# The last batch of a decode kernel passes its second-layer projection and MLP alone, in the form of a turn

## The chip, the cores and the metric

The kernel runs on one core of a Trainium2 chip. The metric is the device time of one execution in microseconds. The core has five engines with queues of their own: PE (matrix multiplication), DVE (vector), ACT (activation functions), POOL (used here for sums over partitions), and SP, which only issues DMA transfers. Inputs lie in HBM and reach the on-chip memory (SBUF) by DMA, over 16 DMA engines; PE writes to PSUM.

## The reference

Two layers are computed one after the other, with the same weights and the same caches in both. A layer is a grouped-query attention block over cached keys and values and a mixer with an MLP, each with a layer norm ahead of it, for 8 batches with one new token each:

```
x = x + A(layernorm(x));  x = x + B(layernorm(x))     # first layer
x = x + A(layernorm(x));  x = x + B(layernorm(x))     # second layer

A: q = x @ wq                       # 448 -> 16 heads x 256
   scores = q . k / 16              # 8 KV heads, two query heads each, 4096 cached tokens
   o = softmax(scores) . v
   return o.reshape(16 * 256) @ wo  # 4096 -> 448
B: ...                              # mixer part: with one token its shifted terms are all zero,
                                    #   so x1 = x
   return x1 + gelu(layernorm(x1) @ w3) @ w4          # 448 -> 1792 -> 448
```

With a sequence of one token each of the mixer's four shifted groups is padded to nothing, so `w1` and `w2` don't touch the output. The batches don't depend on one another. One batch and KV head has 2 MB of keys and 2 MB of values in bfloat16; all of K and V is 256 MB.

## The kernel before

**Slots and loads.** The caches stream through 31 slots of 512 KB (`NSLOT`, 128 partitions of 4 KB). A KV head's keys or values are four chunks of one slot each. `chunks` (L452 to 468) makes the load units: up to `most` neighbouring chunks go in one DMA, so a load has 512 KB, 1 MB or 2 MB, and each partition's part of it is one contiguous row of 4, 8 or 16 KB. All of these loads are issued by SP in one order, `stream`, and each waits until its slots have been read out.

**Pairs of heads.** The work is cut into pairs of KV heads `m` = 0 to 3 of batch `b` in layer 0 or 1. `kpart` computes the scores of a pair: keys are turned either by PE with an eviction by ACT (L856, L916), or by DVE as 32x32 squares (L938); then PE multiplies them with the queries (L926 for the first form, L947 for the second, L975 and L979 for the wide form, which pair 0 of layer 1 has). A softmax over the pair follows (L1004 to L1054), with sums over partitions by POOL. `vpart` passes the values: in the usual form the probabilities are the stationary operand (L1115, with the collecting steps L1126, L1128, L1137, L1141); in the `still` form, used for the last pair of a batch, the values are stationary (L1089, 16 matmuls for each chunk), and the result of each head is normalised by one DVE step (L1096).

**Queries on the diagonal.** For keys turned in squares the queries are needed in a spread form. `diagonal` (L619 to 650) makes it for each pair: a DVE step (`spread`, L633) multiplies eight columns of queries by a mask of quarters, PE sums over partitions with four matmuls of 8 columns each (L640), and another DVE step (`put`, L646) writes the spread queries to one of the two halves of `qe`.

**Turns.** Layer 1 of a batch follows its layer 0 closely: the turned keys of pairs 1 to 3 stay in their slots for it, while pair 0's keys and all values are loaded a second time. Once a batch has all its four pairs of layer 0, `turn(b)` (L652 to 718) takes it to layer 1: output projection (`outproj`, L1155: for each head 16 matmuls of one column, L1163), the residual, the norm (`norm1`, L557), the first MLP layer (`project`, L576: 56 matmuls, L584 and L586), gelu (`gelu`, L590), the second layer (`down`, L602: 56 matmuls, L609), the residual (L678), then the norm and the query projection of layer 1. All of it is for one batch, with one column per operand; scratch lies in `qe` and `small`, and sums in the first columns of the PSUM tile `psT`. Then layer 1 of that batch begins, while the next batch's layer 0 streams.

**The end.** The outputs of layer 1 of all batches gather in `qo`, eight columns (batches) for each head. `outproj8` (L1170) projects a pair for all eight batches at once: 32 matmuls of 8 columns (L1178), called when the last batch's pair has been passed. `end` (L788 to 829) then does the rest for all batches at once: sum of the projections (L797 to 803), `norm8` (L738: L746 to L755), `project` with 8 columns, two roots, `gelu`, `down`, the residual (L814), four transposes back to rows (L821), a copy (L826) and one store of 8 rows (L827). Its scratch is one slot, `U_s1`, handed out after the last load of the stream has its slots.

**Order.** The order on each engine is written by a planner (`Plan.schedule`, L170): every step is an `Op` with an estimated cost, a priority and its dependencies, and the planner lets each engine take the ready step with the lowest priority value. Steps on the same PSUM tile keep the order in which they were added whenever the engine changes. The planner also places the loads: it may split a load of several chunks (`split`, L147) when too few neighbouring slots are free and its estimate of the queue runs low. `end` is added last, with `plan.prio = 1e9`.

For the last batch, `b` = 7, the values go in the order of the pairs 1, 2, 3, 0 (L1267, L1275); pairs 2 and 3 are loaded with up to 2 MB in a DMA, pair 0 with up to 1 MB.

Of the kernel before, what the change touches and what calls it, by code (L numbers as in the profile page):

```python
# [3 lines left out]
P = 128  # L4
B = 8
D = 448
# [354 lines left out]
def bass_interleave_layers__gqa_block_cached__mixer_s_mlp__decode_kernel(  # L361
# [90 lines left out]
    def chunks(cache, b, h, name, skip=(), most=2):  # L452
# [123 lines left out]
    def project(w, wt, half, j0, j1, rhs, out0, nb, units, bufs, name, cost=None):  # L576


        def emit(e):
            last = None  # L580
            for j in range(j0, j1):
                o = psT[:, out0 + j * nb:out0 + (j + 1) * nb]
# [36 lines left out]
    def diagonal(layer, b, m):  # L619
# [11 lines left out]
        def spread(e):  # L631
            src = psT[:, 64 + 8 * m:72 + 8 * m] if layer else qo[:, 8 * m:8 * m + 8, b]
            return e.tensor_tensor(qm.rearrange("p (q x) -> p q x", q=4), src.unsqueeze(1).to_broadcast([P, 4, 8]),  # L633
                                   quarter.unsqueeze(2).to_broadcast([P, 4, 8]), ALU.mult)
        dve(spread, 180, [Bsel] + ([] if layer else [Bq1[b]]), Bqe[k], [bT] if layer else [], name=n + "m")

        def emit(e):
            for c in range(2):
                for h in range(2):
                    last = e.matmul(part.rearrange("p (n c q h) -> p c h q n", c=2, q=4, h=2)[:, c, h],  # L640
                                    same[:, :], qm.rearrange("p (q n h c) -> p c h q n", q=4, h=2, c=2)[:, c, h], start=True, stop=True)
            return last
        add("pe", emit, 140, Bqe[k] + [Bsel], [], [bT], name=n + "s")
# [8 lines left out]
    def turn(b):  # L652

        n = f"turn{b}"
        keep, plan.prio = plan.prio, -1.0
# [3 lines left out]
        last = ahead[[a[0] for a in ahead].index(b)]  # L659
        ahead.remove(last)  # L660
        dve(lambda e: e.tensor_reduce(sjk[:, :], psT[:, 0:24].rearrange("p (s c) -> p c s", c=4), axis=AX.X, op=ALU.add),
            180, [], [Bs["jk"]], [bT], name=n + "ao")
        dve(lambda e: e.tensor_tensor(sjk[:, :], sjk[:, :], x[:, 0:4], ALU.add), 150, [Bs["jk"], Bx[b]], [Bs["jk"]], name=n + "xa")
        outproj(*last, [0])
        dve(lambda e: e.tensor_tensor(sjk[:, :], psT[:, 24:28], sjk[:, :], ALU.add), 150, [Bs["jk"]], [Bs["jk"]], [bT], name=n + "xb")
        plan.turn = True
        outproj(*last, [1])
        dve(lambda e: e.tensor_tensor(sx1[:, 0:4], psT[:, 28:32], sjk[:, :], ALU.add), 150, [Bs["jk"]], [Bs["x1"]], [bT], name=n + "x1")
# [11 lines left out]

        norm1(x, Bx[b], Bx4[b], 41, n + "b")
# [21 lines left out]
        def columns(r):  # L703
            def emit(e):
                for j in range(4):
                    last = e.matmul(psT[:, 64 + 16 * r:80 + 16 * r].rearrange("p (g j) -> p j g", j=4)[:, j],
# [61 lines left out]
    def start():  # L768
# [12 lines left out]
        for i in range(4):  # L781
            project(wq_sb, wqt_sb, 16, 8 * i, 8 * i + 8, rhs, 64, 8, U_wq + wq_rest + [U_s0], [byn], f"sq{i}")
# [5 lines left out]
    def end():  # L788
        w = Wide(U_s1)
# [7 lines left out]
        dve(lambda e: e.tensor_reduce(ao(), psT[:, 0:192].rearrange("p (s c) -> p c s", c=32), axis=AX.X, op=ALU.add),  # L797
            400, [], [bao], [bT], units=u, name="eao")
        dve(lambda e: e.tensor_tensor(ao(), ao(), xT[:, 0:4, :].rearrange("p c b -> p (c b)"), ALU.add), 200, [bao] + Bx, [bao], units=u, name="exa")
# [3 lines left out]
        dve(lambda e: e.tensor_tensor(x1()[:, 0:32], psT[:, 224:256], ao(), ALU.add), 200, [bao, b1], [b1], [bT], units=u, name="ex1")  # L803
# [23 lines left out]
        U_out = plan.load(Unit("out", lambda e, _: e.dma_start(out[:, 0, :], xo()[0:B, :]), 8192, slotted=False),  # L827
# [597 lines left out]
```

## Time and profile before

| | before |
|---|---|
| median of 3 runs | 1095.2 us (1094.35 to 1099.57) |
| the profiled execution | 1096.3 us, its span 1094.5 us |
| PE busy | 764.3 us (70%), 15416 matmuls |
| DVE busy | 830.5 us (76%) |
| ACT, POOL busy | 212.2 us (19%), 72.0 us (7%) |
| moved by DMA | 448.96 MB, mean 410 GB/s |
| mean granted TensorE clock | 0.616 |

The profile is that of one execution. Its span runs from the first to the last recorded instruction, and the execution's own time is 1.8 us longer. "Busy" counts the time in which an engine worked on an instruction; weight loads of PE (PEld) overlap its matmuls. In the timelines the first column is the start in microseconds from the span's start, the second the length; square brackets give the idle time of the engine before it and who ended it. A line number is that of the kernel before.

### The profile page before, as it was taken

The page shows a single profiled execution, that of the slowest core. Times are in us where ns is not written, and L with a number is a line of the kernel's source. Part 1 is how long each engine was busy: PE and PEld are TensorE (multiplying, and loading weights), DVE is VectorE, ACT ScalarE, POOL GpSimd, SP SyncE. Part 2 cuts the span into 40 slices and gives each one's busy share as a digit, 9 for nine tenths or more (in the row PEclk, how much of TensorE's full clock was granted, in tenths as well). Part 3 has the DMA queues.
Part 4 walks back from the last instruction along what each step waited for, and adds up shares of the span by engine and source line. Part 5 has one row for each costly group of instructions (what it writes and reads, how often), then busy time and mean ns, then how long its engine had stood idle before and what let it go on. Part 6 is the DMA issues. An engine that isn't in the chain of part 4 may idle for free.

```text
span 1094.5 us, 33709 instructions
## 1 busy us (share of the span) xinstructions
PE 764.3 (70%) x15416; PEld 525.1 (48%) x15416; DVE 830.5 (76%) x1567; ACT 212.2 (19%) x322; POOL 72.0 (7%) x232
## 2 busy tenths in 40 slices
PE   3467586778677865778667786578766795676865
PEld 3255453465346543565336654365433654346533
DVE  5899549964997499954999569974799839996572
ACT  1023131113011311203202032121221231111310
POOL 0000000000000000000000010000100000000000
PEclk9998566556655665556655566555565666655655
DMA  9999999999999999999999999999999999999994
GB/s 357 405 420 417 411 400 428 422 404 409 428 422 417 411 428 426 422 395 423 426 426 419 399 423 426 426 416 398 427 428 424 400 406 426 426 423 414 416 425 188
DMA packets 54703, 448.96 MB, mean 410 GB/s; under 512 B 5520, under 2 KB 11552, under 8 KB 14112
## 3 DMA queue, kind: packets, MB, share of 16 engines
q1 hardware_dynamic: 54400, 446.42, 98.3%
q8 instruction: 121, 1.98, 0.7%
q10 hardware_dynamic: 160, 0.38, 0.1%
q14 instruction: 22, 0.18, 0.0%
HBM read 446.77 MB, written 0.01 MB: 408 GB/s over the span
## 4 chain that ended last, share of the span: by engine, by line
DVE 39%; DMA 26%; PE 20%; issue 7%; ACT 3%; POOL 1%; SPq 0%; DVEq 0%; POOLq 0%
DVE slots L938 31%; DMA slots<-in_A_k_cache_dram 17%; DMA slots<-in_A_v_cache_dram 9%; PE psV L1115 5%; PE psS L947 4%; DVE pT L1045 2%; PE psS L926 2%; PE psV L1089 2%; PE psT L609 1%; ACT slots L916 1%; DVE slots L1128 1%; PE psT L695 1%; PE psT L1163 1%; PE psK L856 1%; ACT slots L1217 1%
## 5 line engine op out<-in xcount | busy, mean ns | idle before, releaser
L938 DVE STREAM_TRANSPOSE slots<-slots 128x1024 bf16<-128x1024 bf16 x544 | 647.7, 1230 | 38.2 <-DMA slots<-in_A_k_cache_dram 25.1
L947 PE MATMUL psS<-qe,slots 128*128 128x8 bf16 x5760 | 225.4, 174 | 165.2 <-DVE slots L938 107.5
L947 PEld LDWEIGHTS psS<-qe,slots 128*128 128x128 bf16 x5760 | 190.5, 103 | 250.1 <-DVE slots L938 173.0
L1115 PE MATMUL psV<-slots,pT 128*8 128x512 bf16 x1528 | 183.7, 555 | 20.0 <-DMA slots<-in_A_v_cache_dram 15.2
L916 ACT COPY slots<-psK 128x1024 bf16<-128x1024 bf16 x80 | 78.6, 1015 | 165.1 <-PE psK L856 164.6
L856 PE MATMUL psK<-ident,slots 128*128 128x128 bf16 x640 | 75.1, 304 | 3.1 <-DMA slots<-in_A_k_cache_dram 2.9
L1009 POOL PARTITION_ALL_REDUCE small<-small x64 | 23.9, 374 | 720.4 <-DVE small L1007 586.0
L1126 ACT ACTIVATE slots<-psV 128x512 bf16<-128x512 f32 x48 | 28.8, 600 | 201.9 <-PE psV L1115 201.9
L856 PEld LDWEIGHTS psK<-ident,slots 128*128 128x128 bf16 x640 | 62.4, 141 | 5.7 <-DMA slots<-in_A_k_cache_dram 3.5
L975 PE MATMUL psS<-slots,qe 128*8 128x512 bf16 x200 | 55.3, 593 | 6.5 <-DVE slots L938 6.4
L1089 PE MATMUL psV<-pT,slots 128*128 128x2 bf16 x1568 | 50.6, 165 | 9.6 <-DMA slots<-in_A_v_cache_dram 9.0
L1115 PEld LDWEIGHTS psV<-slots,pT 128*8 128x8 bf16 x1528 | 31.5, 90 | 52.6 <-DMA slots<-in_A_v_cache_dram 21.5
L1089 PEld LDWEIGHTS psV<-pT,slots 128*128 128x128 bf16 x1568 | 47.2, 104 | 11.6 <-DMA slots<-in_A_v_cache_dram 9.1
L1128 DVE TENSOR_TENSOR slots<-psV,slots 128x512 bf16<-128x512 f32 x48 | 32.5, 677 | 25.2 <-ACT slots L1126 25.0
L1030 ACT ACTIVATE pT<-psS 128x128 bf16<-128x128 f32 x56 | 15.6, 279 | 173.6 <-DVE psS L1027 173.4
L1045 DVE STREAM_TRANSPOSE pT<-psS 128x128 bf16<-128x128 bf16 x64 | 45.2, 706 | 4.4 <-PE psS L1037 2.2
L1137 PE MATMUL psV<-same,slots 128*128 128x4 bf16 x320 | 14.2, 166 | 41.9 <-DVE slots L1128 36.8
L1163 PE MATMUL psT<-small,wo_sb 128*128 128x1 bf16 x1024 | 35.7, 166 | 7.1 <-DVE small L1096 4.7
L926 PE MATMUL psS<-qo,slots 128*128 128x2 bf16 x768 | 28.0, 167 | 13.4 <-ACT slots L916 10.4
L1163 PEld LDWEIGHTS psT<-small,wo_sb 128*128 128x128 bf16 x1024 | 32.5, 105 | 9.2 <-DVE small L1096 6.0
L1137 PEld LDWEIGHTS psV<-same,slots 128*128 128x128 bf16 x320 | 11.8, 103 | 49.6 <-issue 42.3
L1096 DVE TENSOR_TENSOR small<-psV,small 128x4 bf16<-128x4 f32 x30 | 4.3, 144 | 41.1 <-PE psV L1089 41.1
(178 smaller groups left out, 768.8 us busy)
## 6 DMA issues: line engine op xcount, KB each, us to landing
slots<-in_A_v_cache_dram SPq DMA_DIRECT2D x149, 1024.0 KB, 9.9
slots<-in_A_v_cache_dram SPq DMA_DIRECT2D x50, 2048.0 KB, 21.1
slots<-in_A_k_cache_dram SPq DMA_DIRECT2D x45, 2048.0 KB, 21.1
slots<-in_A_k_cache_dram SPq DMA_DIRECT2D x69, 1024.0 KB, 14.3
slots<-in_A_v_cache_dram SPq DMA_DIRECT2D x14, 512.0 KB, 8.0
wo_sb<-in_A_wo_dram SPq DMA_DIRECT2D x4, 896.0 KB, 19.1
wq_sb<-in_A_wq_dram SPq DMA_DIRECT2D x3, 1024.0 KB, 11.3
w_sb<-in_B_w_dram SPq DMA_DIRECT2D x1, 1568.0 KB, 15.2
```

The costliest lines, as they stand in the source:

```text
L856: last = e.transpose(tile[:, j * P:(j + 1) * P], slots[u.slot][:, o:o + P], ident[:, :])
L916: return e.copy(slots[u.slot][:, 1024 * t:1024 * t + 1024], tile)
L926: last = e.matmul(o, slots[u.slot][:, i:i + P], q, start=(cc == 0), stop=(cc == 1))
L938: return e.transpose(o, i)
L947: last = e.matmul(o, slots[u.slot][:, i:i + P], qe[:, 128 * k + 64 * s + 8 * g:128 * k + 64 * s + 8 * g + 8], start=(g == 0), stop=(g == 7))
L975: last = e.matmul(o, q, K[:, lo:hi + 1:hi - lo, :, g, :], start=(g == 0), stop=(g == 7))
L1045: add("dve", lambda e: e.transpose(pZ[:, :, 0:3:2].rearrange("p n s r -> p n r s"), psS[x][:, 128:192].bitcast(bf).rearrange("p (n r s) -> ...
L1089: last = e.matmul(o, slots[u.slot][:, i:i + P], w, start=(c == 0 and cc == 0 and j == 0), stop=(c == NCH - 1 and cc == 1 and j == 7))
L1115: last = e.matmul(psV[x][32 * i:32 * i + 8, :].rearrange("p (k d) -> p k d", k=2), w, v, start=(s == 0 and c == 0), stop=(s == 1 and c == ...
L1126: add("act", lambda e: e.activation(part(0), psV[x][:, :], ACT.Copy), 590, [], [Bhalf[0]], [bV[x]], [v], prio=at - 1, name=n + "ve0").targ ...
L1128: add("dve", lambda e: e.tensor_tensor(part(1), psV[x][:, :], part(0), ALU.subtract), 590, [Bhalf[0]], [Bhalf[1]], [bV[x]], [v], prio=at - ...
L1163: last = e.matmul(psT[:, 4 * (2 * s + i) + c:4 * (2 * s + i) + c + 1], wo_sb[:, a, d0:d0 + P], o1[b % 2][:, a:a + 1], start=(k == 0), stop ...
```

## The change

The second layer's projection and MLP, so far done in `end` for eight batches at the very end, are cut in two.

- `end` now takes its projection by `outproj8` for all four pairs in one place, and is called before the last batch's pairs 2, 3 and 0 are passed, with priority -0.7 in place of 1e9. It still works on eight columns; the last one holds nothing of use then, and only 7 rows are stored. It hands back its scratch slot.
- The last batch's outputs are projected by `outproj` with one column, read from `qo`, to columns of `psT` from `LAST` = 448 on. The body of `turn` up to the residual becomes the function `block`, with a base column, and the new function `end1` calls it for batch 7, transposes the result back to a row, copies it and stores it. SP waits for both stores.
- In `chunks`, the second head of pair 0 of the last batch is loaded in four DMAs of 512 KB instead of two of 1 MB.
- `diagonal` sums with one matmul of 32 columns instead of four of 8. For that the columns of the queries are kept in another order within each four (`swapped`), and `spread` writes its product in another order. The planner's cost of the step goes from 140 to 60.

```diff
-            if len(group) == most:
+            if len(group) == most and not name.startswith(f"B{B - 1}m0V1"):
                 plan.load(group[0], mates=group[1:])
...
+    def swapped(j):
+        return j // 4 * 4 + j % 2 * 2 + j // 2 % 2
...
-            return e.tensor_tensor(qm.rearrange("p (q x) -> p q x", q=4), src.unsqueeze(1).to_broadcast([P, 4, 8]),
-                                   quarter.unsqueeze(2).to_broadcast([P, 4, 8]), ALU.mult)
+            return e.tensor_tensor(qm.rearrange("p (x q h) -> p x q h", x=4, q=4),
+                                   src.rearrange("p (x h) -> p x h", h=2).unsqueeze(2).to_broadcast([P, 4, 4, 2]),
+                                   quarter.unsqueeze(1).unsqueeze(3).to_broadcast([P, 4, 4, 2]), ALU.mult)
...
-            for c in range(2):
-                for h in range(2):
-                    last = e.matmul(part.rearrange("p (n c q h) -> p c h q n", c=2, q=4, h=2)[:, c, h],
-                                    same[:, :], qm.rearrange("p (q n h c) -> p c h q n", q=4, h=2, c=2)[:, c, h], start=True, stop=True)
-            return last
-        add("pe", emit, 140, Bqe[k] + [Bsel], [], [bT], name=n + "s")
+            return e.matmul(part, same[:, :], qm, start=True, stop=True)
+        add("pe", emit, 60, Bqe[k] + [Bsel], [], [bT], name=n + "s", n=1)
...
-    def turn(b):
+    def block(b, n, last, base):
...
-        outproj(*last, [0])
+        outproj(*last, [0], base)
...
+    def turn(b):
+        n = f"turn{b}"
+        keep, plan.prio = plan.prio, -1.0
+        x = xT[:, :, b]
+        last = ahead[[a[0] for a in ahead].index(b)]
+        ahead.remove(last)
+        block(b, n, last, 0)
...
-        outproj8(*late, [0])
-        dve(lambda e: e.tensor_tensor(ao(), psT[:, 192:224], ao(), ALU.add), 200, [bao], [bao], [bT], units=u, name="exb")
-        outproj8(*late, [1])
+        for m in range(HKV // 2):
+            outproj8(m, m, plan.prio)
...
-        U_out = plan.load(Unit("out", lambda e, _: e.dma_start(out[:, 0, :], xo()[0:B, :]), 8192, slotted=False),
-                          after=bxo.writers)
-        return U_out
+        late.append(plan.load(Unit("out", lambda e, _: e.dma_start(out[0:B - 1, 0, :], xo()[0:B - 1, :]), 7168, slotted=False),
+                              after=bxo.writers))
+        return w
+
+    def end1(w, last):
+        plan.prio = -1.0
+        block(B - 1, "f", last, LAST)
+        xo, bxo = w.tile(bf, D), Buf()
+        def back(e):
+            for cc in (3, 0, 1, 2):
+                d0 = cc * P if cc < 3 else D - P
+                t = e.transpose(psT[0:1, 0:224].bitcast(bf)[:, d0:d0 + P], xT[:, cc, B - 1:B], ident[:, :])
+            return t
+        add("pe", back, 400, [Bx[B - 1], Bc], [], [bT], name="fback", n=4)
+        dve(lambda e: e.tensor_copy(xo()[0:1, :], psT[0:1, 0:224].bitcast(bf)), 450, [], [bxo], [bT], units=[U_s1], name="fxo")
+        late.append(plan.load(Unit("outl", lambda e, _: e.dma_start(out[B - 1:B, 0, :], xo()[0:1, :]), 1024, slotted=False),
+                              after=bxo.writers))
...
-                q = q.rearrange("p (s c) -> p s c", c=2)[:, :, cc]
+                q = q[:, 2 * cc:2 * cc + 2]
...
-                late.extend((m, s, at[0] + 1))
+                late.append((b, m, s, -0.5))
             else:
-                outproj8(m, s, at[0] + 1)
+                outproj(b, m, s, at[0] + 1, (0, 1), LAST)
...
+            keep, plan.prio = plan.prio, -0.7
+            W = end()
+            plan.prio = keep
             for m in (2, 3, 0):
                 weave(V(1, b, m, most=4 if m else 2))
-    plan.prio = 1e9
-    U_out = end()
+    end1(W, next(x for x in late if isinstance(x, tuple)))
```

More of the change, by code (lines that the diff above doesn't have):

```diff
@@ L574, in norm1, with project @@
         root(lambda: sf[:, 2:3], lambda k: sf[:, (1, 1, 3, 4)[k]:(2, 2, 4, 5)[k]], None, [Bs["sq"]], [Bs["f"]], [], name + "n", True)
-    def project(w, wt, half, j0, j1, rhs, out0, nb, units, bufs, name, cost=None):
+    def swapped(j):
+        return j // 4 * 4 + j % 2 * 2 + j // 2 % 2
+    def project(w, wt, half, j0, j1, rhs, out0, nb, units, bufs, name, place=lambda j: j):
         def emit(e):
@@ L581, in emit @@
             for j in range(j0, j1):
-                o = psT[:, out0 + j * nb:out0 + (j + 1) * nb]
+                o = psT[:, out0 + place(j) * nb:out0 + (place(j) + 1) * nb]
                 for k in range(3):
@@ L705, in emit @@
                 for j in range(4):
-                    last = e.matmul(psT[:, 64 + 16 * r:80 + 16 * r].rearrange("p (g j) -> p j g", j=4)[:, j],
+                    last = e.matmul(psT[:, 64 + 16 * r:80 + 16 * r].rearrange("p (g j) -> p j g", j=4)[:, swapped(j)],
                                     slots[v.slot][:, 512 * r + P * j:512 * r + P * j + P],
@@ L1162, in emit @@
                         a = 8 * m + 4 * i + k
-                        last = e.matmul(psT[:, 4 * (2 * s + i) + c:4 * (2 * s + i) + c + 1], wo_sb[:, a, d0:d0 + P],
-                                        o1[b % 2][:, a:a + 1], start=(k == 0), stop=(k == 3))
-                return last
-            add("pe", emit, 430, [Bo1[b % 2][m][i]], [], [bT], U_wo, prio=prio, name=f"W{b}m{m}{i}", n=16)
-    late = []
+                        last = e.matmul(psT[:, base + 4 * (2 * s + i) + c:base + 4 * (2 * s + i) + c + 1], wo_sb[:, a, d0:d0 + P],
+                                        qo[:, a, b:b + 1] if base else o1[b % 2][:, a:a + 1], start=(k == 0), stop=(k == 3))
+                return last
+            add("pe", emit, 430, [Bo2[m][i] if base else Bo1[b % 2][m][i]], [], [bT], U_wo, prio=prio, name=f"{'WX'[base > 0]}{b}m{m}{i}", n=16)
+    late, LAST = [], 448
     def outproj8(m, s, prio, heads=(0, 1)):
@@ L1273, in bass_interleave_layers__gqa_block_cached__mixer_s_mlp__decode_kernel @@
         else:
+            keep, plan.prio = plan.prio, -0.7
+            W = end()
+            plan.prio = keep
             for m in (2, 3, 0):
                 weave(V(1, b, m, most=4 if m else 2))
-    plan.prio = 1e9
-    U_out = end()
+    end1(W, next(x for x in late if isinstance(x, tuple)))
+    U_out = [x for x in late if not isinstance(x, tuple)]
     order = U_side[:1] + U_even[:1] + U_side[1:] + U_even[1:] + [U_s0] + stream[:1] + U_wq + stream[1:10] + U_wo + stream[10:]
     order.append(U_s1)
-    order.append(U_out)
+    order += U_out
     seq = plan.schedule(order, NSLOT)
@@ L1374, in run @@
         if e == "sp":
-            eng.wait_ge(U_out.sem, U_out.val)
+            for u in U_out:
+                eng.wait_ge(u.sem, u.val)
     with nc.Block() as blk:
```

25 lines of the change are left out of this document (10 added, 15 removed).

## The prediction

> **What bounds the kernel now.** I read the page first, then the windows of the last 45 us, then the timeline of the end, and last the timeline of a turn, because the change puts a turn's form at the end.
>
> ```profile
> span 1094.5 us, 33709 instructions
> ...
> PE 764.3 (70%) x15416; PEld 525.1 (48%) x15416; DVE 830.5 (76%) x1567; ACT 212.2 (19%) x322; POOL 72.0 (7%) x232
> ...
> DMA  9999999999999999999999999999999999999994
> ...
> DVE 39%; DMA 26%; PE 20%; issue 7%; ACT 3%; POOL 1%; SPq 0%; DVEq 0%; POOLq 0%
> ```
>
> The 16 DMA engines are busy in tenths of 9 in every slice but the last, while PE is at 70%. So the kernel is one stream of cache loads, and its time is the moment at which the last load lands plus what must still be computed after it. The chain names DVE first, but where the stream is never dry a DVE step only matters if it keeps a load from being issued.
>
> The windows show how the stream ends (columns: window, length, busy us of PE, weight loads, DVE, ACT and POOL with their counts, granted clock, DMA share, GB/s):
>
> ```profile
> core 0: us, PE busy (x) PEld busy (x) DVE busy (x) ACT busy (x) POOL busy (x), PEclk, DMA share, GB/s
> 1050.00:1057.00 7.00, 2.51 (x28) 0.77 (x28) 6.91 (x8) 0.96 (x3) 0.00 (x0) 0.50 1.01 426
> 1057.00:1065.00 8.00, 7.21 (x97) 3.70 (x93) 2.26 (x8) 1.06 (x3) 0.83 (x3) 0.69 1.00 426
> 1065.00:1075.00 10.00, 4.38 (x72) 1.81 (x72) 1.18 (x4) 0.93 (x2) 0.07 (x1) 0.69 1.00 419
> 1075.00:1082.50 7.50, 4.73 (x152) 4.42 (x152) 1.80 (x6) 0.16 (x1) 0.00 (x0) 0.50 0.59 244
> 1082.50:1092.80 10.30, 5.78 (x168) 5.07 (x168) 4.93 (x33) 0.30 (x1) 0.41 (x1) 0.50 0.01 4
> ```
>
> The DMA share is 1.00 until 1075 and 0.59 in the 7.5 us after; in the last 10.3 us the DMA is idle (0.01) and PE, DVE and one ACT step take turns. That last stretch is what the change is about. A share of 0.59 with loads still landing also says that some engines are through before others, so the last landing is that of the slowest. In the timeline of it (start, length, engine, line, operation, count, idle before and releaser):
>
> ```profile
> 1080.05 1.01 PE L1089 MATMUL psV<-pT,slots 128*128 128x2 bf16 x32 [0.56 <-DMA slots<-in_A_v_cache_dram]
> ...
> 1082.51 1.01 PE L1089 MATMUL psV<-pT,slots 128*128 128x2 bf16 x32 [1.44 <-DMA slots<-in_A_v_cache_dram]
> 1083.55 0.18 DVE L1096 TENSOR_TENSOR qo<-psV,small 128x4 bf16<-128x4 f32 x1 [3.77 <-PE psV L1089]
> ...
> 1083.79 0.59 PE L1178 MATMUL psT<-qo,wo_sb 128*128 128x8 bf16 x16 [0.27 <-DVE qo L1096]
> 1084.49 0.19 DVE L803 TENSOR_TENSOR slots<-psT,slots 128x32 bf16<-128x32 f32 x1 [0.75 <-PE psT L1178]
> ...
> 1089.80 1.66 PE L609 MATMUL psT<-slots,w_sb 128*128 128x8 bf16 x56 [2.60 <-DVE slots L599]
> 1091.49 0.19 DVE L814 SCALAR_TENSOR_TENSOR slots<-psT,slots 128x32 bf16<-128x32 f32 x1 [1.75 <-PE psT L609]
> ...
> 1091.74 0.59 PE L821 MATMUL psT<-ident,slots 128*8 128x128 bf16 x4 [0.28 <-DVE slots L814]
> 1092.36 0.38 DVE L826 COPY slots<-psT 8x448 bf16<-8x448 bf16 x1 [0.68 <-PE psT L821]
> 1092.82 0.31 SPq L827 DMA_DIRECT2D out_dram<-slots  x1
> ```
>
> The last two megabytes of V are passed at 1080.05 and 1082.51, each waiting for its DMA; the landings are 2.46 us apart. After the last one everything is a single chain: 32 matmuls of the last pass, the normalisation by the softmax sum (L1096), 16 matmuls of the output projection (L1178), the sum (L803), norm and first MLP layer, the second layer (L609), the residual (L814), four transposes, a copy and the store. From 1082.51 to the end of the span at 1094.5 this tail is 12.0 us, 1.1% of the time. No edit of the tail alone can bring more than that.
>
> **Part 1, the tail in a turn's form.** The kernel already runs this chain for one batch in every turn. Here is the last turn (PE rows of L1163 are the output projection, L609 the second MLP layer, L678 the residual):
>
> ```profile
> 1013.02 0.16 DVE L1096 TENSOR_TENSOR small<-psV,small 128x4 bf16<-128x4 f32 x1 [3.17 <-PE psV L1089]
> ...
> 1013.24 0.58 PE L1163 MATMUL psT<-small,wo_sb 128*128 128x1 bf16 x16 [0.26 <-DVE small L1096]
> ...
> 1013.75 0.60 PE L1115 MATMUL psV<-slots,pT 128*8 128x512 bf16 x4
> ...
> 1014.28 0.27 PE L531 MATMUL psT<-qe,small 128*128 128x1 bf16 x4
> ...
> ```
>
> ```profile
> 1018.18 1.65 PE L609 MATMUL psT<-qe,w_sb 128*128 128x1 bf16 x56 [0.23 <-DVE qe L599]
> ...
> 1019.87 0.18 DVE L678 SCALAR_TENSOR_TENSOR small<-psT,qe 128x4 bf16<-128x4 f32 x1 [1.75 <-PE psT L609]
> ```
>
> From L1096 to the residual the turn takes 1019.87 - 1013.02 = 6.85 us; the eight-batch form takes 1091.49 - 1083.55 = 7.94 us. The difference is 1.09 us. It comes from fewer and shorter DVE steps (128x1 in place of 128x8, a scalar operand in place of a broadcast one); the second layer's 56 matmuls are no shorter (1.65 against 1.66), so PE gives nothing here. In the turn another pass of 4 matmuls (1013.75) lies ahead of L531 and costs at most 0.1 us, which the end doesn't have; I leave it as slack. After the residual the steps stay: four transposes (now one row instead of eight, still 128 columns each), a copy of 448 columns, a store; 1094.5 - 1091.49 = 3.01 us, taken unchanged. Term: **-1.1 us**, between -1.2 (slack gained) and -0.6 (half of it lost to steps placed otherwise).
>
> **Part 2, the last head's V in four loads.** The last load is now half as large, so after the last landing 16 matmuls remain instead of 32. By the row at 1082.51 the 32 take 1.01 us, some 27 ns each beyond the first (0.17 by the median of a single small matmul below), so 16 fewer are **-0.4 us**. Against it stands what smaller packets cost in the stream. Each load is one row per partition, so 2 MB that went as 8 KB packets now go as 4 KB packets (512 of them). One answer per window of 4 us, each with its count under 8 KB: calm (994), the three with many 4 KB packets (1010, 486, 878), and one with none that is slow all the same (866):
>
> ```profile
> DMA packets 231, 1.67 MB, mean 418 GB/s; under 512 B 28, under 2 KB 28, under 8 KB 28
> ```
>
> ```profile
> DMA packets 287, 1.54 MB, mean 384 GB/s; under 512 B 33, under 2 KB 33, under 8 KB 168
> ```
>
> ```profile
> DMA packets 266, 1.41 MB, mean 351 GB/s; under 512 B 35, under 2 KB 35, under 8 KB 156
> ```
>
> ```profile
> DMA packets 357, 1.59 MB, mean 398 GB/s; under 512 B 42, under 2 KB 42, under 8 KB 285
> ```
>
> ```profile
> DMA packets 193, 1.38 MB, mean 344 GB/s; under 512 B 25, under 2 KB 25, under 8 KB 25
> ```
>
> Calm is 418 GB/s. The window at 878 holds 285 - 42 = 243 packets of 4 KB (1.0 MB) and loses 20 of 418, 0.19 us per MB, so 0.4 us for 2.1 MB. The one at 1010, the nearest in time, holds 135 and loses 34 of 418 over 4 us, 0.33 us for 0.55 MB, which would be 1.2 us. The one at 486 holds 121 and would give 2.7 us. But 866 falls to 344 with not one such packet, so part of each dip is the turn's and not the packets'. The lower end is nothing. I take **+0.4 us**, from the window with most such packets, and keep 0 to 1.2 for the range and 2.7 for a rival. The two further issues, the split 2 MB load and the second store lie on SP, which issues nothing between the last load and the store at 1092.82: nothing, and with that cover gone 0.3 us each.
>
> **Part 3, batches 0 to 6 earlier.** What was the tail for eight columns is now run beside the last loads, and the last batch's projections are made anew for one column: 128 more matmuls (four times the 1.0 us of 32 such) and, by the last window, 5.78 - 1.01 - 0.59 = 4.2 us of PE and 4.9 us of DVE that come ahead of the last landing. In the instruction order of the changed kernel 96 of those matmuls stand ahead of the last batch's final transposes' scores, near 1040 to 1045, the rest and the norm from the last batch's wide scores on, after 1057. From 1057 to 1082.5 PE is busy 7.21 + 4.38 + 4.73 of 25.5 us and DVE 5.24 of 25.5: 9.2 us and 20 us are free. What could be late next are the loads: those that wait for a slot behind these steps. The last of them is already in the queue long before:
>
> ```profile
> slots<-in_A_v_cache_dram SPq DMA_DIRECT2D x1, 1024.0 KB, 29.6
> ```
>
> It is issued 29.6 us ahead of its landing, so a release that comes 1 to 3 us later (3 us of PE at 1040, one DVE memset that waits for PE) is swallowed. The other thing behind the moved steps is the last softmax, whose chain shares DVE and PE with them:
>
> ```profile
> 1061.05 0.69 DVE L1004 TENSOR_REDUCE small<-psS 128x1 f32<-128x512 f32 x1 [3.61 <-PE psS L979]
> ...
> 1064.56 0.72 DVE L1045 STREAM_TRANSPOSE pT<-psS 128x128 bf16<-128x128 bf16 x1
> ...
> ```
>
> ```profile
> 1075.21 0.99 PE L1089 MATMUL psV<-pT,slots 128*128 128x2 bf16 x32 [0.70 <-DMA slots<-in_A_v_cache_dram]
> ```
>
> It ends at 1065.3 and is first needed at 1075.21; some ten DVE steps of 0.2 us and 56 matmuls of 1.7 us in its way use 4 of these 10 us. Term: **0**; without that cover it would be up to 4.2 us of PE work.
>
> **Part 4, the diagonal.** One matmul of 32 columns takes the place of four of 8, in 64 places, and the spreading step gets a view of four dimensions:
>
> ```profile
> L640 PE MATMUL psT<-qe,same x256: 169/174/221, 25.2 to 1038.9; 128*128 128x8 bf16 x128
> ```
>
> ```profile
> L633 DVE TENSOR_TENSOR qe<-psT,small x32: 151/192/193, 148.3 to 1038.6; 128x32 bf16<-128x32 f32 x32
> ```
>
> ```profile
> L646 DVE TENSOR_TENSOR qe<-psT,small x64: 250/292/442, 26.2 to 1040.0; 128x128 bf16<-128x128 f32 x64
> ```
>
> On PE that is three of 174 ns fewer, pipelined 0.10 us, 64 times: 6.7 us off an engine with 30% idle. On DVE the step of 0.19 us stays between its present minimum 0.15 and the 0.29 of the wider four-dimensional step. Only in the turns are two such chains in series with the queries, so at most 8 x 2 x 0.1 = 1.6 us, if the stream followed every turn. But its loads are held by passes and score matmuls of many kinds, so I take **0**, with -1.6 and (0.1 us lost on DVE in the same 16 places) +1.6 as ends. The planner also orders some steps otherwise from the first batch on, since it counts this step as shorter; I price that as a rival.
>
> **Sum.** -1.1 - 0.4 + 0.4 + 0 + 0 = -1.1 us. The profiled execution took 1096.3 us (span 1094.5 and 1.8 around it), 1.1 above the median of the three runs, 1095.2. On the profile's own time the sum gives 1095.2, and on the median **1094.1**.
>
> **Rivals.** First, on the other side: the small loads cost more than they save. The place is the last 2 MB, the price 2.7 us by the window at 486, and from 1.5 us on it cancels the whole gain. That ends at 1095.2 - 1.5 + 2.7 = 1096.4, slower than before. Against it: the landings at 1080.05 and 1082.51 are as far apart as 1 MB at 418 to 428 GB/s needs, so a queued load shows no price of its own. The Trainium skill speaks against this edit in "DMA: Bandwidth & Descriptors", section "Measured (HBM→SBUF, 128 partitions, SWDGE, issued from GpSimd)": loads should be batched to 1 MiB or more, and the fit in that page's section "Anatomy of one DMA — SWDGE (gpsimd) path" gives each transfer about 2.0 us beside its bytes. By that fit as an estimate two more loads would be +4 us and the kernel would end at 1097.7. The trace's 2.46 us per queued megabyte doesn't bear the fixed part out.
>
> Second: the new order lets the queue of loads run thinner in the turns. A dip as at 866 costs 4 x (418 - 344) / 418 = 0.7 us; one more in four of eight turns is 2.8 us, 1096.9. For it: these dips exist. Against: nearly all loads keep their sizes and places in SP's order.
>
> Third: the turns follow the shorter diagonal and the new order helps. With the full 1.6 us it is 1092.5.
>
> Fourth: the change doesn't do what it says, because the work for batches 0 to 6 is still in PE's and DVE's queues when the last load lands. Up to 4.2 us come back, 1098.3. Against it are the free 9.2 us of PE, and that after each landing PE needs 1.0 of 2.46 us, so a backlog shrinks.
>
> **How the numbers follow.** Forecast 0.60 (1093.0 to 1095.3, from the ends of parts 1 and 2), small loads 0.12, thinner queue 0.11, quicker turns 0.12, late work 0.05. The likeliest gives 1094.1. The range takes in the first three rivals and leaves out late work and mishaps beyond them: 1091.5 to 1097.3. A change of 0.5%, 5.5 us, is about what a measurement of this kernel can tell from nothing; the gain is a fifth of that. Below 1089.7 only a turn effect three times the bound would lead: 0.03. Above 1100.7 only late work together with thinner queues: 0.04. That leaves 0.93.
>
> **What would show it.** Right: the store is issued 8.6 to 9.2 us after the start of the last pass (now 1092.82 - 1082.51 = 10.31); the last pass has 16 matmuls; from the last normalisation by the softmax sum to the residual it takes 6.7 to 6.9 us; the copy of rows 0 to 6 ends before the last landing; the last landing stays within 1 us of 1082.5. Wrong: the last landing moves by more than 1.5 us either way, a pass starts late with its data landed, or the windows of the turns show other GB/s. Then it is the stream and not the tail that decided.

## The result, and the profile after

| | before | after |
|---|---|---|
| median | 1095.42 us (21 runs, 1094.32 to 1100.16) | 1092.94 us (21 runs, 1092.07 to 1095.14) |
| ratio | | 0.9977, 95% interval 0.9969 to 0.9985 |
| the profiled execution | 1096.3 us, span 1094.5 | 1092.74 us, span 1090.9 |

The change takes 2.5 us off (1.6 to 3.4 by the interval), 0.23%. The forecast was a gain of 1.1 us. The lines of the page, the windows of the end and the timeline of the tail, all of the changed kernel, in the columns told ahead of the prediction's:

```profile
span 1090.9 us, 33799 instructions
...
PE 767.1 (70%) x15448; PEld 523.3 (48%) x15448; DVE 834.3 (76%) x1597; ACT 212.4 (19%) x323; POOL 72.2 (7%) x233
...
DVE 34%; DMA 32%; PE 21%; issue 6%; SPq 4%; ACT 3%; POOL 0%; DVEq 0%; POOLq 0%
```

```profile
1050.00:1057.00 7.00, 2.55 (x55) 1.18 (x48) 6.45 (x10) 0.99 (x3) 0.01 (x1) 0.94 0.99 413
1057.00:1065.00 8.00, 8.00 (x132) 4.79 (x130) 3.06 (x15) 0.95 (x2) 0.58 (x2) 0.50 1.02 433
1065.00:1075.00 10.00, 9.53 (x199) 5.73 (x196) 4.84 (x30) 1.49 (x3) 0.77 (x3) 0.50 0.99 407
1075.00:1082.50 7.50, 5.26 (x179) 5.01 (x178) 1.89 (x8) 0.00 (x0) 0.00 (x0) 0.50 0.36 143
1082.50:1092.80 10.30, 4.16 (x120) 3.62 (x120) 3.48 (x26) 0.21 (x1) 0.40 (x1) 0.50 0.01 2
```

```profile
1066.13 0.74 DVE L1067 STREAM_TRANSPOSE pT<-psS 128x128 bf16<-128x128 bf16 x1
...
1072.46 0.31 SPq L833 DMA_DIRECT2D out_dram<-slots  x1
...
1074.23 0.72 PE L1111 MATMUL psV<-pT,slots 128*128 128x2 bf16 x21
...
1075.52 0.43 PE L1111 MATMUL psV<-pT,slots 128*128 128x2 bf16 x11 [0.57 <-issue]
...
1078.61 0.48 PE L1111 MATMUL psV<-pT,slots 128*128 128x2 bf16 x13
...
1080.34 1.09 PE L1111 MATMUL psV<-pT,slots 128*128 128x2 bf16 x35 [1.24 <-issue]
1081.47 0.18 DVE L1118 TENSOR_TENSOR qo<-psV,small 128x4 bf16<-128x4 f32 x1 [2.45 <-PE psV L1111]
...
1081.70 0.58 PE L1185 MATMUL psT<-qo,wo_sb 128*128 128x1 bf16 x16 [0.27 <-DVE qo L1118]
...
1086.43 1.66 PE L613 MATMUL psT<-qe,w_sb 128*128 128x1 bf16 x56 [1.43 <-DVE qe L603]
1088.12 0.17 DVE L677 SCALAR_TENSOR_TENSOR small<-psT,qe 128x4 bf16<-128x4 f32 x1 [1.75 <-PE psT L613]
...
1088.35 0.59 PE L846 MATMUL psT<-ident,small 128*1 128x128 bf16 x4 [0.27 <-DVE small L677]
1088.98 0.38 DVE L849 COPY slots<-psT 1x448 bf16<-1x448 bf16 x1 [0.68 <-PE psT L846]
1089.38 0.25 SPq L850 DMA_DIRECT2D out_dram<-slots  x1
```

Lines have moved with the edit: L1111 is now the last pass (L1089), L1118 the normalisation by the softmax sum (L1096), L1185 the output projection of one batch, L613 the second MLP layer, L677 the residual, L1067 the last softmax's final step (L1045).

From the normalisation (1081.47) to the residual (1088.12) it takes 6.65 us, where the eight-batch form took 7.94 and the turn 6.85. From the residual to the end of the span it is 2.78 us instead of 3.01. So the chain behind the last pass is 1.52 us shorter. The rows of batches 0 to 6 are stored at 1072.46, well ahead of the last landing. PE's busy time between 1057 and 1075 went from 11.6 to 17.5 us and DVE's from 3.4 to 7.9: that is the moved work. But the span is 3.6 us shorter, so about 2 us lie ahead of the chain. Windows of half a microsecond show when the stream ends, first in the kernel before, then in the changed one (the last column is GB/s):

```profile
1081.50:1082.00 0.50, 0.00 (x0) 0.00 (x0) 0.00 (x0) 0.00 (x0) 0.00 (x0) 0.50 0.04 16
1082.00:1082.50 0.50, 0.00 (x0) 0.00 (x0) 0.00 (x0) 0.00 (x0) 0.00 (x0) 0.50 0.00 0
```

```profile
1079.00:1079.50 0.50, 0.10 (x4) 0.01 (x1) 0.02 (x1) 0.00 (x0) 0.00 (x0) 0.50 0.04 16
1079.50:1080.00 0.50, 0.00 (x0) 0.00 (x0) 0.00 (x0) 0.00 (x0) 0.00 (x0) 0.50 0.00 0
```

In these two executions the stream ended about 2.5 us sooner. With the 1.5 us of the chain that would be 4.0; some 0.4 us of it is missing, and PE stood still for 1.24 us ahead of 1080.34.

### The profile page after: what moved, and what is told of

Its sections match the earlier page's. It is cut to its first block, busy times and chain, and to the rows that moved or that the text cites. A ratio compares the mean times of both kernels' runs of the same rounds, so it can differ in the third digit from the quotient of the medians.

```text
span 1090.9 us, 33799 instructions
## 1 busy us (share of the span) xinstructions
PE 767.1 (70%) x15448; PEld 523.3 (48%) x15448; DVE 834.3 (76%) x1597; ACT 212.4 (19%) x323; POOL 72.2 (7%) x233
## 4 chain that ended last, share of the span: by engine, by line
DVE 34%; DMA 32%; PE 21%; issue 6%; SPq 4%; ACT 3%; POOL 0%; DVEq 0%; POOLq 0%
DVE slots L960 26%; DMA slots<-in_A_k_cache_dram 20%; DMA slots<-in_A_v_cache_dram 13%; PE psV L1137 6%; PE psS L969 4%; SPq L434 3%; DVE pT L1067 2%; PE psS L948 1%; PE psV L1111 1%; ACT slots L938 1%; DVE slots L1150 1%; PE psT L613 1%; PE psT L702 1%; PE psS L997 1%; SPq L459 1%
## 5 line engine op out<-in xcount | busy, mean ns | idle before, releaser
L1111 PE MATMUL psV<-pT,slots 128*128 128x2 bf16 x1568 | 50.8, 165 | 7.3 <-DMA slots<-in_A_v_cache_dram 5.0
L1111 PEld LDWEIGHTS psV<-pT,slots 128*128 128x128 bf16 x1568 | 47.4, 104 | 8.8 <-DMA slots<-in_A_v_cache_dram 5.9
L1067 DVE STREAM_TRANSPOSE pT<-psS 128x128 bf16<-128x128 bf16 x64 | 45.4, 710 | 5.2 <-PE psS L1059 2.8
L1185 PE MATMUL psT<-small,wo_sb 128*128 128x1 bf16 x1024 | 35.1, 166 | 7.1 <-DVE small L1118 5.1
L638 DVE TENSOR_TENSOR qe<-psT,small 128x32 bf16<-128x32 f32 x32 | 5.9, 185 | 41.6 <-PE psS L969 37.0
L1185 PEld LDWEIGHTS psT<-small,wo_sb 128*128 128x128 bf16 x1024 | 32.1, 104 | 9.3 <-DVE small L1118 6.4
```

The costliest lines, as they stand in the source:

```text
L1067: add("dve", lambda e: e.transpose(pZ[:, :, 0:3:2].rearrange("p n s r -> p n r s"), psS[x][:, 128:192].bitcast(bf).rearrange("p (n r s) -> ...
L1111: last = e.matmul(o, slots[u.slot][:, i:i + P], w, start=(c == 0 and cc == 0 and j == 0), stop=(c == NCH - 1 and cc == 1 and j == 7))
L1185: last = e.matmul(psT[:, base + 4 * (2 * s + i) + c:base + 4 * (2 * s + i) + c + 1], wo_sb[:, a, d0:d0 + P], qo[:, a, b:b + 1] if base els ...
```

## The experiments

Times are given against the kernel before, run on the same chip; a ratio of 0.999 is 1.1 us.

### The whole change again, and without the new diagonal

Run e1_after_again is the changed kernel unedited. Run e2_old_diagonal takes the diagonal back and leaves the rest:

```diff
-            return e.matmul(part, same[:, :], qm, start=True, stop=True)
-        add("pe", emit, 60, Bqe[k] + [Bsel], [], [bT], name=n + "s", n=1)
+            for c in range(2):
+                for h in range(2):
+                    last = e.matmul(part.rearrange("p (n c q h) -> p c h q n", c=2, q=4, h=2)[:, c, h],
+                                    same[:, :], qm.rearrange("p (q n h c) -> p c h q n", q=4, h=2, c=2)[:, c, h], start=True, stop=True)
+            return last
+        add("pe", emit, 140, Bqe[k] + [Bsel], [], [bT], name=n + "s")
```

The views of `spread` and of the scores and the order of the columns go back too.

> The changed kernel as it is, beside the others on one chip, as the yardstick. Both theories expect 2.5 us below the kernel before (ratio 0.9977). In its profile: from the last normalisation by the softmax sum to the end of the span 9.4 us where the kernel before has 10.95.

> The changed kernel with the diagonal as before: four matmuls of 8 columns, the old order of columns and the planner's old cost; the new tail and the four small loads stay. Tail theory (the gain is the shorter chain after the last landing, 1.5 us, and the half pass, 0.4 us, the rest is chance): 1.9 to 2.5 us below the kernel before, the same as the yardstick within 0.5 us. Stream theory (the tail gives 1.9 us less a price of the small loads, and the diagonal with the planner's new order brings the stream forward by 1 us or more in the turns): only 0.9 to 1.5 us below the kernel before, 1 us or more above the yardstick.

Measured: e1 0.9973 (0.9963 to 0.9984), median 1092.97; e2 0.9984 (0.9973 to 0.9994), median 1093.92, 1.8 us below the kernel before. Tail and loads carry a good part of the gain, and without the diagonal about 1 us of it is missing. The 1.8 us lie just under what the tail theory expected (1.9 to 2.5), and the distance to e1, 1.2 us by the ratios and 1.0 by the medians, is what the stream theory expected; the two intervals overlap. In e1 it is 9.5 us from the last normalisation (1080.75) to the end of the span, where 9.4 was expected.

### The new diagonal alone, its order and its step apart

Three runs start from the kernel before. e3_diagonal_only has the new diagonal and the planner's new cost; e5_new_diagonal_old_order has the new instructions with the old cost, which gives the old order on every engine; e6_planner_cost_only has the old instructions with the new cost, which gives the order of e3:

```diff
 e3: new views, one matmul
-        add("pe", emit, 140, Bqe[k] + [Bsel], [], [bT], name=n + "s")
+        add("pe", emit, 60, Bqe[k] + [Bsel], [], [bT], name=n + "s", n=1)
 e5: new views, one matmul; the line of add as before
 e6: old views, four matmuls; the line of add as in e3
```

> The kernel before with the new diagonal alone (one matmul of 32 columns, the new order of columns, the planner's new cost); tail and loads as before. Tail theory: no change, within 0.4 us of the kernel before. Stream theory: 0.8 to 1.6 us below it, and in its profile the norms of the turns come 1.5 to 3 us sooner, as in the changed kernel.

> The kernel before with the new diagonal's instructions, but the planner keeps its old cost, so every engine's order is the old one. The new diagonal with the planner's new cost alone gained about 2 us. If that gain is the shorter step itself (three small matmuls fewer in the turns, at most 1.6 us), this run has it too: 1.0 to 2.0 us below the kernel before. If it is the order, this run is within 0.5 us of the kernel before.

> The kernel before with its old diagonal of four matmuls, but the planner counts it as 60 and one matmul, so the order on every engine is that of the run with the new diagonal alone. If the order is what gained there: 1.0 to 2.0 us below the kernel before. If the shorter step: within 0.5 us of the kernel before, or above it by the 0.1 us of each step that the planner now doesn't count.

Measured: e3 0.9982 (0.9973 to 0.9990), 2.0 us below; e5 0.9983 (0.9973 to 0.9992), 1.9 us below; e6 1.0023 (1.0010 to 1.0036), 2.5 us above. In the traces DVE, ACT and POOL run through the same sequence of steps in e6 as in e3, and in e5 as in the kernel before, so the orders are those that the text says. The new instructions gain by themselves, in either order. The order gains nothing: with the old instructions behind it, it loses.

Where the stream gained can be read from a fixed point near its end, the sum over partitions of the last turn's second norm. It is the same POOL step in the kernel before, e5, e2 and the changed kernel, one row each:

```profile
1021.34 0.40 POOL L572 PARTITION_ALL_REDUCE small<-small  x1 [5.61 <-DVE small L568]
```

```profile
1019.66 0.40 POOL L572 PARTITION_ALL_REDUCE small<-small  x1 [5.64 <-DVE small L568]
```

```profile
1021.65 0.40 POOL L572 PARTITION_ALL_REDUCE small<-small  x1 [5.60 <-DVE small L568]
```

```profile
1018.45 0.40 POOL L572 PARTITION_ALL_REDUCE small<-small  x1 [5.86 <-DVE small L568]
```

With the new diagonal it comes 1.7 us (e5) and 2.9 us (changed) sooner, with the old diagonal in the changed kernel no sooner (e2, 0.3 later). In e3 it comes at 1019.41, 1.9 us sooner, as the stream theory expected. Over all executions, the four kernels with the old diagonal have this step at 1021.17 or later, and six of the seven whose diagonals all have one matmul have it between 1018.45 and 1019.66; the seventh is e12, the run with many small loads below, with 1021.08. Each is a single execution, so one row proves nothing alone.

The view of SP's own waits shows where the diagonal can hold up a load (what SP waited for, us in total, times, longest). In the kernel before and in e5, spread, sum and put of the diagonal:

```profile
SPq L459 <- DVE qe L646: 24.0, 5, 5.5
SPq L459 <- DVE qe L633: 19.5, 4, 5.5
...
SPq L459 <- PE psT L640: 10.0, 9, 3.5
```

```profile
SPq L459 <- DVE qe L647: 21.6, 5, 5.7
...
SPq L459 <- DVE qe L637: 15.3, 4, 4.5
SPq L459 <- PE psT L643: 10.6, 9, 3.4
```

In the kernel before 53.5 us of waiting ahead of 18 loads ended with a step of the diagonal. In e5 it is 47.5 us for 18. But this sum doesn't follow the time: in e6, the slowest kernel of all, it is 41.0 us for 17 loads, and in e11 below, 0.7 us under the kernel before, it is 48.6 us for 18. So that the loads leave sooner because of these waits is not shown.

### Which diagonals, and how many matmuls

The changed kernel with the one matmul cut into four for one layer, and the kernel e5 with it cut into eight (the comment is not in the kernels; it tells them apart):

```diff
-            return e.matmul(part, same[:, :], qm, start=True, stop=True)
+            if layer:                      # e9; e10: if not layer; e11, on e5: always, 8 of 4 columns
+                for i in range(4):
+                    last = e.matmul(part[:, 8 * i:8 * i + 8], same[:, :], qm[:, 8 * i:8 * i + 8], start=True, stop=True)
+                return last
+            return e.matmul(part, same[:, :], qm, start=True, stop=True)
```

> The changed kernel with the diagonal's matmul cut into four of 8 columns again, for the diagonals of layer 1 alone (32 places, two of them in series in each turn); views, orders and the planner's cost as changed. Turn theory (the shorter step gains where it stands in a turn's chain): it loses the diagonal's gain, 1 to 2 us above the changed kernel. Everywhere theory (each of the 64 steps can hold up a load): half of it, 0.5 to 1 us above. If the views and not the number of matmuls gained: no change.

> The same for the diagonals of layer 0 alone (the other 32 places, none in a turn's chain). Turn theory: no change against the changed kernel, within 0.4 us. Everywhere theory: 0.5 to 1 us above it. If the views gained: no change in this run and none in the one for layer 1.

> The kernel before with the new views, the old order and the diagonal's sum in eight matmuls of 4 columns, where the kernel before has four of 8 and the run with one matmul in the old order was 1.9 us below it. If the number of matmuls sets the gain, about 0.09 us a step for three: four more cost about 2.3 us above the kernel before. If the views set it: 1.9 us below the kernel before, as with one matmul.

Measured: e9 0.9977 (0.9966 to 0.9988), the ratio of the changed kernel; e10 0.9990 (0.9980 to 1.0000), 1.4 us above it between the points (each distance has an interval of about 1.5 us either way); by the medians, 1093.40 and 1094.26, e10 is 0.9 us above e9; e11 0.9994 (0.9985 to 1.0003), 0.7 us below the kernel before, where 2.3 us above was expected from the count and 1.9 below from the views.

The turn theory isn't borne out: layer 1's steps, two of which stand in each turn's chain, lost nothing that this run can see, where 1 to 2 us were expected; the lower end of that is not shut out. What was lost was lost in layer 0, though the intervals of e9 and e10 overlap. The count of matmuls is not the whole cause either, since eight are no slower than the old four. Some rows of the steps, of e5, of the kernel before and of e11:

```profile
L643 PE MATMUL psT<-qe,same x64: 176/190/234, 24.0 to 1039.2; 128*128 128x32 bf16 x64
...
L637 DVE TENSOR_TENSOR qe<-qo,small x32: 145/172/375, 23.8 to 973.8; 128x32 bf16<-128x32 bf16 x32
```

```profile
L633 DVE TENSOR_TENSOR qe<-qo,small x32: 164/194/378, 25.0 to 976.2; 128x32 bf16<-128x32 bf16 x32
```

```profile
L645 PE MATMUL psT<-qe,same x512: 164/166/213, 24.4 to 1040.0; 128*128 128x4 bf16 x171
```

One matmul of 32 columns takes 190 ns by its median, hardly more than one of 8 columns (174). All the diagonal's matmuls together, of the kernel before and of e5 (busy time in us, mean of one in ns):

```profile
L640 PE MATMUL psT<-qe,same 128*128 128x8 bf16 x256 | 16.7, 175 | 3.5 <-DVE qe L633 3.3
```

```profile
L643 PE MATMUL psT<-qe,same 128*128 128x32 bf16 x64 | 12.4, 194 | 6.4 <-DVE qe L637 6.2
```

So the step is 4.3 us shorter over 64 places, 0.07 us each. Layer 0's spreading step, which reads `qo`, went from 194 to 172 ns with the new view, 32 times: 0.7 us of DVE, and only of layer 0 (in e6, with the old view, it took 185 ns, which leaves 0.4 us). That can be a part of what e11 kept, but not the reason of e10, which has the new view and still lost. No run has the new views with four matmuls in both layers, so how the 1.9 us divide between views and count stays open.

### The small loads

e4_two_loads is the changed kernel with the condition on the name taken out of `chunks`; e7_small_loads_only is the kernel before with the condition; e12_many_small_loads widens it to pairs 2, 3 and 0:

```diff
-            if len(group) == most and not name.startswith(f"B{B - 1}m0V1"):
+            if len(group) == most and not (name.startswith(f"B{B - 1}m") and "V" in name and name[3] != "1"):
```

> The changed kernel with the last head's V in two loads of 1 MB again; all else as changed. If the smaller packets cost nothing, the last pass has 32 matmuls again and the time is 0.4 us above the yardstick. If they cost what I took (0.4 us), it is the same as the yardstick. If they cost 1.2 us or more (the upper end), it is 0.8 us or more below the yardstick.

> The kernel before with the last head's V in four loads of 512 KB and nothing else. If smaller packets cost nothing, 0.4 us below the kernel before (half a pass less after the last landing); if they cost the 0.4 us I took, no change; if 1.2 us or more, 0.8 us or more above it. The profile shows the last pass with 16 matmuls in place of 32 in each case.

> The changed kernel with all V of the last batch's pairs 2, 3 and 0 in loads of 512 KB, 12 MB in place of 2 MB. At the price I took (0.2 us for each MB in smaller packets) it is 2 us above the changed kernel; at the upper end of 0.6 us for each MB, 6 us above it; if smaller packets cost nothing, the same within 0.4 us.

Measured: e4 0.9975 (0.9964 to 0.9985), the same as the changed kernel; e7 1.0003 (0.9993 to 1.0014), no change; e12 0.9977 (0.9965 to 0.9988), the same as the changed kernel, with six times the small loads. The timelines say why. The end of the last passes in e7, then the last four in e12:

```profile
1081.23 0.59 PE L1089 MATMUL psV<-pT,slots 128*128 128x2 bf16 x16 [0.63 <-DMA slots<-in_A_v_cache_dram]
...
1082.42 0.59 PE L1089 MATMUL psV<-pT,slots 128*128 128x2 bf16 x16 [0.61 <-DMA slots<-in_A_v_cache_dram]
1083.05 0.18 DVE L1096 TENSOR_TENSOR qo<-psV,small 128x4 bf16<-128x4 f32 x1 [2.96 <-PE psV L1089]
```

```profile
1079.42 0.58 PE L1111 MATMUL psV<-pT,slots 128*128 128x2 bf16 x16 [0.70 <-DMA slots<-in_A_v_cache_dram]
...
1080.66 0.58 PE L1111 MATMUL psV<-pT,slots 128*128 128x2 bf16 x16 [0.23 <-DMA slots<-in_A_v_cache_dram]
1082.16 0.59 PE L1111 MATMUL psV<-pT,slots 128*128 128x2 bf16 x16 [0.92 <-DMA slots<-in_A_v_cache_dram]
1083.39 0.59 PE L1111 MATMUL psV<-pT,slots 128*128 128x2 bf16 x16 [0.65 <-DMA slots<-in_A_v_cache_dram]
```

In e7 the 512 KB loads are passed 1.19 us apart, which is 2.4 us for each MB, as with the 1 MB loads (2.46). In e12 the four stand 1.24, 1.50 and 1.23 us apart. A smaller packet has no price here that these runs can see: 10 MB more of them cost 0 with an interval of about 1.5 us either way, where I had put 2 us. The half pass is also seen in e7: normalisation 0.63 us after the start of the last pass, not 1.04. That 0.4 us is too little for the intervals of e4 and e7. By the Trainium skill's "DMA: Bandwidth & Descriptors" (the 2.0 us of each transfer in "Anatomy of one DMA — SWDGE (gpsimd) path") e12's ten more megabytes, 13 more loads by the two profiles, would as an estimate have cost over 20 us if each load paid it in turn. These runs don't agree with that: queued behind other loads, nothing of the kind was paid.

### The moved work

e8_no_early_work is the changed kernel without the steps of `end` between the scratch tiles and the copy:

```diff
-        (projection, sum, norm, both MLP layers, residual and transposes of `end`)
-        dve(lambda e: e.tensor_copy(xo()[0:B, :], psT[0:B, 0:224].bitcast(bf)), 450, [], [bxo], [bT], units=u, name="exo")
+        dve(lambda e: e.memset(xo()[0:B, :], 0.0), 100, [], [bxo], units=u, name="exo")
```

> The changed kernel without the second layer's projection and MLP of batches 0 to 6: that part is left out and zeros are stored for these rows, so only the last batch's row is computed to the end. Hidden-work theory (my price of 0 for the moved work): the same as the changed kernel within 0.5 us, 2.5 us below the kernel before. Late-work theory (the moved steps hold up loads or the last softmax): 1 us or more below the changed kernel, and its last landing or last pass comes sooner in the profile.

Measured: 0.9974 (0.9963 to 0.9985), the changed kernel's own value. The moved work is hidden, as far as an interval of about 1.5 us either way can tell; the late-work theory expected 1 us or more.

## Why the prediction came out as it did

The direction and the range were right (1091.5 to 1097.3; 1092.94 measured). The size was under half of what came, and of the four parts one was mis-sized. By the prediction's own signs the mechanism was half right. The chain took 6.65 us where 6.7 to 6.9 was the sign, and the rows of batches 0 to 6 were copied ahead of the last landing. But the stream ended 2.5 us sooner, more than the 1.5 us that was named as the sign of the stream, and not the tail, deciding.

**Part 1, the turn's form: right, and a little low.** The term was -1.1 us. The chain from the normalisation to the residual fell by 1.29 us: the 1.09 read from the turn and 0.20 more, where I had granted the turn 0.1 of slack for the pass beside it. The end after the residual was taken unchanged and fell by 0.23 us (the store's issue alone 0.31 to 0.25). Together 1.5 us.

**Part 2, the small loads: the sum right, both terms off.** The half pass is worth the 0.4 us I gave it where PE waits for the landing, as in e7. The price of smaller packets, 0.4 us from the window at 878, isn't there: e12 shows none. Those windows must then have dipped for another reason, as the one at 866 already said, and I should have taken the lower end. That the sum of the two terms came out near what e4 and e7 show is luck, within their noise. In the changed kernel's own profile the half pass wasn't gained: PE stood still for 1.24 us with no wait the profile shows, ahead of 35 matmuls (1080.34) that then ran without a gap, while the DMA moved nothing from 1079.5 on, so the last two loads had landed before they were needed. The rival that had the small loads cancel the gain falls with e7 and e12.

**Part 3, the moved work: right.** e8 takes it away and gains nothing. The last softmax ended at 1066.87 in place of 1065.28 and was first needed at 1074.23; 7.4 of the 10 us of cover were left.

**Part 4, the diagonal: this step failed.** I took 0, because the loads are "held by passes and score matmuls of many kinds", and gave a bound of 1.6 us for the turns. Alone it is worth 1.9 to 2.0 us (e3, e5), and the place was probably wrong as well: the chain that I priced, two steps in each turn, lost nothing to be seen when its matmuls were cut again (e9). SP's own waits, which I had read only for the end of the stream, name the diagonal behind 18 loads. I treated the wait table's long rows as the only ones, when the short rows are those that the change touched. The sum on PE was off too: 6.7 us were taken, and the busy time fell by 4.3. The rival "quicker turns" came closest in size, by a mechanism that the runs don't bear out. By which path the shorter step brings the stream forward stays open; the last section has a second candidate.

**The reorder.** The rival "thinner queue" is seen in e6: the same new order, with the old step behind it, costs 2.5 us. Its page and that of the kernel before have these rates in 40 slices of the span (e6 first):

```profile
GB/s 358 402 421 419 411 392 427 422 387 397 427 423 407 382 430 425 423 406 416 427 426 422 395 423 427 427 418 400 424 428 426 413 410 427 427 422 398 417 428 201
```

```profile
GB/s 357 405 420 417 411 400 428 422 404 409 428 422 417 411 428 426 422 395 423 426 426 419 399 423 426 426 416 398 427 428 424 400 406 426 426 423 414 416 425 188
```

In the ninth, tenth and 14th slice, which hold or border on the second and third turn, e6 moves 387, 397 and 382 GB/s instead of 404, 409 and 411; the sum over partitions of the third turn's first norm comes at 364.23 instead of 360.24, and of the last turn's second norm at 1024.62 instead of 1021.34. With the new step behind the same order there is no loss (e3). That the planner's cost and the step must agree for this is the likely reading, but only these two runs bear on it.

The parts don't simply add. Tail and loads without the diagonal gave 1.8 us (e2), the diagonal alone 1.9 (e5), the whole 2.5 to 3.0. Each of these has an interval of about 1.1 us either way, and in the changed kernel's profile PE's gap in the last passes takes some 0.4 us back; which of the two it is stays open.

## What to carry to other kernels

When a kernel is one long stream, read the queue's own waits for the steps that a change touches, also where their rows are small: each can be a load that leaves sooner or later. Take them as a question for a run, not as a price, since here their sum did not follow the time. Price a moved tail from a place where the kernel already runs that form, step by step; that was good to 0.4 us here. Change a planner's cost and the step it stands for together: here the cost alone cost 2.5 us.

## What was not expected of the hardware

In the changed kernel PE stopped in the middle of a pass, after 13 of its 16 matmuls, for 1.24 us; in the second run of the same program it stopped after the same 13, for 0.56 us:

```profile
1078.58 0.48 PE L1111 MATMUL psV<-pT,slots 128*128 128x2 bf16 x13
...
1079.62 1.09 PE L1111 MATMUL psV<-pT,slots 128*128 128x2 bf16 x35 [0.56 <-issue]
```

The profile calls the gap "issue": nothing that it shows ended it. It stands at the same instruction in both executions, and in e4, where the last megabyte is one load, PE also stops after the same 13 (1.14 us), so it isn't tied to the landing. What PE waits for there was not tested, but the traces point at its own instructions. The page of the changed kernel has a queue of its own for instructions:

```profile
q8 instruction: 121, 1.98, 0.7%
```

That is 16.4 KB to a packet, and PE has 15448 matmuls and as many weight loads, so one packet for 255 of its instructions. The stops ahead of 1075.52 and 1080.34 lie 128 matmuls apart, which with their weight loads is 256 instructions. In the traces of all 14 kernels every stop of PE over 0.2 us that is put down to "issue" ends 1.2 to 1.6 us after a packet of this queue has ended.

Such stops are spread over the whole kernel: by the view of PE's waits they add up to 30.4 to 32.6 us in the four kernels with the old diagonal and to 20.1 to 27.3 us in the seven with one matmul. Fewer instructions could thus have gained by this path as well as by the shorter step. It doesn't fit everywhere (e9, as fast as the changed kernel, has 31.3 us, and e11, slower than e5, has 20.0), and no run separates the two.

Smaller loads of 4 KB to a partition streamed as fast as those of 8 KB when they were queued behind other loads (1.19 us for 512 KB against 2.46 for 1 MB), although the three windows of the prediction that hold many such packets are dips of the rate.
